# Weights by whole rows, four chunks first, and a second buffer of sums: a fused attention and feed-forward kernel on one core

## The chip, the cores and the metric

The kernel runs on one core of one Trainium2 chip. The metric is the device time of one execution in microseconds (us). Every comparison runs the changed kernel and the kernel before in turn on the same chip, and gives a 95% interval of the ratio. Faster or slower needs a difference of over 2%. A span is the time from the first to the last instruction of a profiled run. The granted clock is the share of TensorE's full clock that a profile shows as granted. A transfer is moved in packets (of w1, w2 and w3, one row or half row each: the profile before has 1536 packets of 4096 bytes, the half rows of w1 and w2) by the 16 DMA engines whose share the profile shows; a rate worked out from packets is 16 times the bytes of one over its mean time.

## The reference, cut to what matters

```python
# attention: q, k, v, f_logit are (4, 8, 768, 48)
f = 1.0 / (1.0 + np.exp(-f_logit))
for t in range(S):
    state = f[:, :, t, :, None] * state + np.einsum('bhd,bhe->bhde', k[:, :, t], v[:, :, t])
    y[:, :, t] = np.einsum('bhd,bhde->bhe', q[:, :, t], state)
# bridge to x of (3072, 384), then the feed-forward part
a = x @ w1                 # w1, w2: (384, 1024), float64
b = x @ w2
h = a * b @ w3             # w3: (1024, 1024), float64
return (h @ w_out).astype(np.float32)      # w_out: (1024, 384), float64
```

## The kernel before

The kernel works on 24 chunks of 128 tokens (attention) and on six blocks of 512 tokens (feed-forward). It multiplies w3 by w_out once (the "fold", 64 products of 384 columns; the trace has two matmul instructions for each product, 128 for these 64, so its counts are double) and then needs only up products (x with w1 and w2) and down products (a times b with the folded weights). From block 1 or 2 on it uses seven products in place of eight, which needs sums of the quarters of x and of the weights. A planner puts all work in order by priorities: a number given with each piece of work, lower first. This kernel has TensorE write its results into buffers called banks; four of them (f in the trace) serve the folds and the up and down products.

The weights arrive as 64-bit words and are decoded into float32: ScalarE and VectorE take them apart in a "raw" buffer and join them again. The 384 rows of w1 are the features of eight heads of 48. A chunk of rows on the 128 partitions is built of 96 rows from the upper part of the matrix and 32 from its end, so each piece of w1 or w2 needs two transfers, one into partitions 0 to 95 and one into 96 to 127:

```python
top, low = slice(0, 2 * D), slice(2 * D, P)          # 0:96 and 96:128
def source(w, kc0, kc1, half):
    cols = slice(half * NW, half * NW + NW)          # half a row: 512 words, 4096 bytes
    lo = HP * 2 * D - 2 * D
    n = P - 2 * D
    return (
        w[kc0 * 2 * D : kc1 * 2 * D, cols].rearrange("(kc p) c -> p kc c", p=2 * D),
        w[lo + kc0 * n : lo + kc1 * n, cols].rearrange("(kc p) c -> p kc c", p=n),
    )
due = {0: 2.0, 1: 26.0}
...
# the due times of the chunks of attention
return (0.0, 10.0, 22.0, 25.0)[u] if u < 4 else 45.0 + 14.5 * (u - 4)
...
# a leaves its bank into a buffer of its own; one buffer for the sums of x
s["a", jc, c0] = work.tile([P, TB], F32, name="a")
nc.scalar.copy(s["a", jc, c0][:, 0:nt], s["pu", jc, 0, c0][:, 0:nt])
...
xs = at(5120, 4, TH)
...
# a fold leaves its bank on VectorE; the down products rank by their block alone
return lambda: nc.vector.tensor_copy(wc[:, place_of(jc)], w3s["p", jc])
...
n0 = 100 * n + 90 + i
```

w3 and w_out need no split: each of their pieces is one transfer into all 128 partitions.

## Time and profile before

| what | before |
|---|---|
| time, median of 3 (lowest to highest) | 527.6 us (527.56 to 529.46) |
| span of the profiled run, and that same run's time | 528.7, 530.42 us |
| busy TensorE, VectorE, ScalarE, GpSimd | 94, 70, 30, 8% |
| first product of the fold starts | 87.6 us |
| first down product starts | 158.3 us |
| last matmul starts | 522.8 us |
| idle VectorE in the first 66 us | 15.1 us |

The prediction below reads the profile in detail. The list of transfer issues: its columns are the transfer, the queue, the count, the size of one, and the median time from issue to landing in us. These are lines of the kernel before; the list names the matrix of w1, w2 and w3 alike, and 1024 KB pieces are those of w3:

```profile
place<-in_w_dram SPq DMA_DIRECT2D x8, 1024.0 KB, 5.2
...
place<-in_w_dram SPq DMA_DIRECT2D x4, 768.0 KB, 10.4
place<-in_w_out_dram SPq DMA_DIRECT2D x4, 768.0 KB, 4.8
...
place<-in_w_dram SPq DMA_DIRECT2D x4, 384.0 KB, 13.0
```

A 768 KB piece of w_out into 128 partitions landed in 4.8 us; a 768 KB piece of w1 or w2 into 96 partitions took 10.4. The time to landing is more than the transfer's own: in the same list the 384 KB pieces took 13.0 us, longer than the 768 KB ones, so this alone proves nothing, but it is a warning that the length of a row is not the only difference between w1 and w3. The packet records of the same trace say more: the rows of w_out are shorter (3072 bytes), and yet their packets came at 310 GB/s (159 ns on average), those of w1 and w2 at 230.

### The profile page before, as it was taken

To read this page: it belongs to the slowest core of one execution; us is meant where nothing else is said; L and a number is where in the kernel's file an instruction comes from. 1 tells how busy PE (TensorE), PEld (TensorE's weight loads), DVE (VectorE), ACT (ScalarE), POOL (GpSimd) and SP (SyncE) were. 2 spreads that over 40 slices of the span, in tenths; PEclk is the share of its full clock that TensorE was granted. 3 is DMA by queue.
4 is the path that set the end of the run, shared out by engine and by line. 5 is a ranking of instruction groups with operands and counts; after the bars stand their busy time and mean duration, and the time that the engine had idled before them with its cause. 6 is when DMAs were issued, how large, how long until landed. Compare 5 with 4: busy or idle time off the path is not lost.

```text
span 528.7 us, 8629 instructions
## 1 busy us (share of the span) xinstructions
PE 497.6 (94%) x3306; PEld 423.3 (80%) x3306; DVE 369.4 (70%) x693; ACT 157.6 (30%) x328; POOL 40.0 (8%) x44
## 2 busy tenths in 40 slices
PE   3777999999999999999999999999999999999995
PEld 2666985666659988889889888898889888998884
DVE  6687999999998989364886657137673566456561
ACT  3646865663125465211351101401110111011000
POOL 5101001100012212000120000100000000000000
PEclk9988999999999999999999999999999999999999
DMA  6988886754113475000240001200013000000001
GB/s 168 217 215 222 259 262 207 235 197 135 29 47 114 130 223 153 30 1 16 56 141 30 1 0 31 76 30 1 0 30 92 2 0 1 31 30 1 1 17 51
DMA packets 29811, 46.02 MB, mean 87 GB/s; under 512 B 5440, under 2 KB 19264, under 8 KB 28736
## 3 DMA queue, kind: packets, MB, share of 16 engines
q1 hardware_dynamic: 29760, 45.37, 29.9%
q8 instruction: 28, 0.46, 0.4%
q14 instruction: 23, 0.19, 0.1%
HBM read 36.70 MB, written 4.72 MB: 78 GB/s over the span
## 4 chain that ended last, share of the span: by engine, by line
PE 77%; DMA 10%; DVE 5%; SPq 4%; POOL 1%; ACT 1%; issue 1%; DVEq 0%; POOLq 0%; ACTq 0%
PE f L481 57%; PE f L921 8%; DMA place<-in_w_dram 5%; PE pa L338 4%; PE py L382 3%; PE py L388 3%; DMA f<-in_f_logit_dram 2%; SPq L451 2%; PE pk L404 2%; PE pk L364 1%; DVE place L716 1%; DMA vt<-in_v_dram 1%; SPq L448 1%; DMA place<-in_w_out_dram 1%; DVE ab L623 0%
## 5 line engine op out<-in xcount | busy, mean ns | idle before, releaser
L481 PE MATMUL f<-xt,w 128*128 128x256 f32 (+2 forms) x696 | 163.6, 369 | 3.6 <-DVE w L868 3.6
L481 PEld LDWEIGHTS f<-xt,w 128*128 128x128 f32 x696 | 118.7, 194 | 25.3 <-issue 9.6
L481 PE MATMUL f<-place 128*128 128x192 f32 (+1 forms) x504 | 114.1, 350 | 2.9 <-DVE place L716 2.9
L481 PEld LDWEIGHTS f<-place 128*128 128x128 f32 x504 | 87.7, 190 | 9.8 <-DVE place L716 4.1
L353 POOL TENSOR_SCALAR_AFFINE_SELECT A<-A 128x1024 f32<-128x1024 f32 x24 | 33.0, 1374 | 296.5 <-ACT A L347 296.5
L921 PE MATMUL f<-place 128*128 128x384 f32 x128 | 43.0, 489 | 0.0
L584 ACT COPY a<-f 128x256 f32<-128x256 f32 x36 | 13.4, 372 | 97.3 <-PE f L481 96.4
L481 PE MATMUL f<-xt,place 128*128 128x256 f32 x144 | 37.1, 380 | 0.0
L481 PE MATMUL f<-wc,ab 128*128 128x192 f32 x192 | 36.5, 330 | 0.0
L921 PEld LDWEIGHTS f<-place 128*128 128x128 f32 x128 | 23.7, 190 | 15.7 <-issue 0.6
L608 DVE TENSOR_TENSOR place<-f,a 128x256 f32<-128x256 f32 x36 | 15.3, 425 | 28.9 <-PE f L481 28.9
L481 PEld LDWEIGHTS f<-wc,ab 128*128 128x128 f32 x192 | 31.7, 190 | 1.9 <-DVE ab L623 1.2
L338 PE MATMUL pa<-Q,K 48*128 48x128 f32 x384 | 29.8, 297 | 2.5 <-DVE K L329 2.3
L299 DVE TENSOR_TENSOR_SCAN fwd<-gate,floor 112x512 f32<-112x512 f32 x24 | 29.3, 1221 | 3.9 <-ACT gate L291 3.2
L338 PEld LDWEIGHTS pa<-Q,K 48*128 48x128 f32 x384 | 25.1, 199 | 8.6 <-issue 6.3
L321 DVE TENSOR_TENSOR_SCAN bwd<-gate,back 112x512 f32<-112x512 f32 x24 | 31.4, 1308 | 0.8
L382 PE MATMUL py<-A,vt 128*48 128x128 f32 (+1 forms) x384 | 27.9, 288 | 2.4 <-POOL A L353 1.5
L481 PEld LDWEIGHTS f<-xt,place 128*128 128x128 f32 x144 | 27.0, 189 | 3.7
L382 PEld LDWEIGHTS py<-A,vt 128*64 128x64 f32 (+1 forms) x384 | 21.8, 135 | 8.1 <-issue 5.2
L347 ACT COPY A<-pa 128x1024 f32<-128x1024 f32 x24 | 24.2, 1009 | 13.2 <-PE pa L338 13.1
L432 ACT ACTIVATE ys<-py 112x512 f32<-112x512 f32 x24 | 14.3, 596 | 38.0 <-PE py L388 25.4
L850 ACT ACTIVATE place<-place 128x1024 f32<-128x1024 f32 (+1 forms) x18 | 20.0, 1113 | 17.8 <-DMA place<-in_w_dram 9.3
(92 smaller groups left out, 622.3 us busy)
## 6 DMA issues: line engine op xcount, KB each, us to landing
place<-in_w_dram SPq DMA_DIRECT2D x8, 1024.0 KB, 5.2
f<-in_f_logit_dram SPq DMA_DIRECT2D x48, 96.0 KB, 2.8
q<-in_q_dram SPq DMA_DIRECT2D x48, 96.0 KB, 2.9
k<-in_k_dram SPq DMA_DIRECT2D x48, 96.0 KB, 2.8
vt<-in_v_dram SPq DMA_DIRECT2D x24, 192.0 KB, 2.9
out_dram<-o SPq DMA_DIRECT2D x24, 192.0 KB, 1.9
place<-in_w_dram SPq DMA_DIRECT2D x4, 768.0 KB, 10.4
place<-in_w_out_dram SPq DMA_DIRECT2D x4, 768.0 KB, 4.8
```

Of the source, the lines that this page charges most:

```text
L299: nc.vector.tensor_tensor_scan(s["P"], gate[u % 2][:, 0:NQ], floor, 0.0, ALU.mult, ALU.max)
L321: nc.vector.tensor_tensor_scan(s["R"][:, ::-1], gate[u % 2][:, NQ:0:-1], back[:, ::-1], 0.0, ALU.mult, ALU.max)
L338: nc.tensor.matmul(s["pa"][:, par, cols], lhsT=s["K"][rows(par), cols], rhs=s["Q"][rows(par), cols], start=True, stop=True,)
L347: nc.scalar.copy(s["A"].rearrange("p r h c -> p r (h c)"), s["pa"])
L353: nc.gpsimd.affine_select(out=a, in_=a, pattern=[[0, H], [1, C]], compare_op=ALU.is_ge, fill=0.0, base=0, channel_multiplier=-1,)
L382: nc.tensor.matmul(s["py"][64 * par : 64 * par + w, hp], lhsT=s["v"][:, h * D : h * D + w], rhs=s["A"][:, par, hp], start=(hp == 0), stop= ...
L388: nc.tensor.matmul(s["py"][:, hp], lhsT=sb[(u - 1) % 2][:, hp], rhs=s["Q"][:, hp * C : hp * C + C], start=False, stop=True, skip_group_che ...
L432: nc.scalar.activation(s["ys"], s["py"], AF.Copy, accum_out=ysum[:, u : u + 1])
L481: nc.tensor.matmul(out_, lhsT=lhs[i], rhs=rhs[i], start=start and i == 0, stop=i == len(lhs) - 1, skip_group_check=True,)
L608: nc.vector.tensor_tensor(ups["u3", k], q["Y"], q["a"], ALU.add)
L850: nc.scalar.activation(s["m"], s["hi"].bitcast(F32), AF.Abs)
L921: nc.tensor.matmul(w3s["p", jc], lhsT=w3s[jc][:, 0, kc * P : kc * P + P], rhs=wos[:, kc], start=(kc == 0), stop=(kc == KF - 1),)
```

## The change

Its intent: bring w1 and w2 by whole rows of 8192 bytes, have the first four chunks of attention (and so all of block 0's x) ahead of the weights, keep a in the place where the product goes, so that no buffer is waited for, move the copies of the folds to ScalarE, give the sums of x a second buffer, and rank the down products later, so that they run among the next block's up products. The diff, cut to its core:

```diff
-NW = 512
-NPE = 1
+NPE = 4
...
-        return (0.0, 10.0, 22.0, 25.0)[u] if u < 4 else 45.0 + 14.5 * (u - 4)
+        return (0.0, 1.0, 2.0, 3.0)[u] if u < 4 else 45.0 + 14.5 * (u - 4)
...
-    xs = at(5120, 4, TH)
+    xss = [at(a, 4, TH) for a in (5120, 12864)]
...
-                    s["a", jc, c0] = work.tile([P, TB], F32, name="a")
-                    nc.scalar.copy(s["a", jc, c0][:, 0:nt], s["pu", jc, 0, c0][:, 0:nt])
+                return lambda: nc.scalar.copy(a_b(jc)[:, cols], s["pu", jc, 0, c0][:, 0:nt])
...
-                last = [q[nm] for q in upq[-KF:] for nm in ("m5", "m6", "m7", "m3")] if i == 0 else []
+                last = [q[nm] for q in blk[n - 2].get("seven", []) for nm in ("m5", "m6", "m7", "m3")] if i == 0 else []
...
-            for c in range(UB):
-                part(c, c + 1, range(KH))
-            part(0, UB, range(KH, KF))
+            part(0, 2, range(KH))
+            part(2, 4, range(KH))
+            part(0, 4, range(KH, KF))
...
-            n0 = 100 * n + 90 + i
+            n0 = 100 * n + 90 + i + 60 * (n > 1) + 30 * (n == NB - 2)
...
+        for which, w in enumerate((w1, w2)):
+            for kc in range(KM):
+                loads_ = [
+                    (top, w[kc * 2 * D : kc * 2 * D + 2 * D].unsqueeze(1)),
+                    (low, w[lo + kc * n : lo + kc * n + n].unsqueeze(1)),
+                ]
+                ends = fetch(loads_, 1, (-26.0, -16.5)[which] + 0.1 * kc, [
...
-            return lambda: nc.vector.tensor_copy(wc[:, place_of(jc)], w3s["p", jc])
+            return lambda: nc.scalar.copy(wc[:, place_of(jc)], w3s["p", jc])
```

The diff also gives the decoding five raw buffers at first, in place of three, and decodes w1 and w2 in halves of 512 columns.

## The prediction

> **What bounds the kernel now.** I read four views: the busy rows in slices, the table by windows, the chain that ended last, and the gaps between matmuls in the trace. First the slices (40 slices of 13.2 us, busy tenths):
>
> ```profile
> PE   3777999999999999999999999999999999999995
> DVE  6687999999998989364886657137673566456561
> DMA  6988886754113475000240001200013000000001
> ```
>
> Three regimes show. Up to slice 5 (66 us) TensorE is not full while DMA is nearly full. From slice 4 to about slice 14 VectorE is full beside TensorE. After 215 us TensorE alone is full. The windows give the first two regimes in numbers (columns: window, its length, then busy us and instruction count of PE, PEld, DVE, ACT, POOL, then granted clock, DMA share, GB/s):
>
> ```profile
> 0.00:13.00 13.00, 4.01 (x36) 3.37 (x36) 8.87 (x18) 4.68 (x8) 7.19 (x21) 1.00 0.66 167
> 13.00:26.00 13.00, 9.61 (x88) 8.52 (x88) 7.94 (x10) 7.57 (x12) 2.29 (x2) 1.00 1.04 221
> 26.00:40.00 14.00, 9.71 (x75) 9.28 (x76) 12.29 (x20) 6.02 (x13) 0.00 (x0) 0.88 0.83 211
> 40.00:53.00 13.00, 9.56 (x95) 8.54 (x94) 9.58 (x15) 8.79 (x16) 1.79 (x2) 0.87 0.85 224
> 53.00:66.00 13.00, 13.00 (x136) 12.71 (x135) 12.23 (x21) 11.52 (x23) 1.00 (x1) 1.00 0.84 257
> 92.00:105.00 13.00, 12.98 (x88) 8.59 (x87) 12.72 (x18) 7.77 (x11) 1.40 (x1) 1.00 0.73 229
> ```
>
> In the first 66 us VectorE idles 15.1 us (4.1 + 5.1 + 1.7 + 3.4 + 0.8), with the DMA queues at 211 to 257 GB/s. The chain says what it waited for, then shows the PE-bound part (columns: start us, us, what):
>
> ```profile
> 6.46 8.87 DMA place<-in_w_dram
> 15.34 9.51 DMA place<-in_w_dram
> 30.49 9.29 DMA place<-in_w_dram
> ...
> 87.72 5.16 PE f L921 x16
> ...
> 158.41 2.80 PE f L481 x16
> ...
> 389.91 0.70 DVE place L716
> ...
> 448.32 0.70 DVE place L716
> ...
> 505.78 0.70 DVE place L716
> ```
>
> The w1/w2 pieces pace the start; 87.72 is the first product of the weight fold (w3 by w_out), 158.41 the first down product. Later there is only a step on VectorE at each block's end: the sums that the first down product needs.
>
> I then set TensorE's own work against the clock. Spacings between matmuls in the trace are about 0.43 us for 256 columns, 0.32 for 192, 0.85 for 512, 0.23 for 128, 0.645 for the fold's 384; the attention groups take 1.09 (pairs), 0.6 (turn, update), 1.02 (values), 1.06 (carry), from the chain. By these the program's order holds 485.3 us of TensorE work: 60.2 ahead of the first fold, 130.3 ahead of the first down product. So the lag (clock minus work) is 87.7 - 60.2 = 27.5 at the first fold, 158.4 - 130.3 = 28.1 at the first down product, and 523.1 - 485.3 = 37.8 at the last matmul; 5.6 us of evictions and store follow. Nearly three quarters of the lag is made before 66 us.
>
> [...] up to 130 us the 4096-byte packets of w1/w2 took 285 ns on average, the 8192-byte ones of w3 372 ns. On 16 engines that is 230 against 352 GB/s. [...] 949 ns for 768 and 1216 for 1024 elements of the sign step leave a fixed 148 ns. [...] Here four gaps of 0.90 us (at 321.7, 389.6, 448.0, 505.5) repeat, but they wait for operands rather than space.
>
> **The change part by part.**
>
> 1. Whole rows. w1/w2 are 6.29 MB: 1536 packets x 285 ns / 16 = 27.4 us of all engines become 768 x 372 / 16 = 17.9, so 9.5 us less DMA time in the stage that DMA limits. The decoding is in halves of 512: by the two-point fits 0.43 + 0.43 + 0.68 + 0.68 = 2.2 us each instead of 3.8 per 1024, which is 12 x 2.2 - 6 x 3.8 = 3.6 us more VectorE work (2.8 by spacing).
>
> 2. First four chunks ahead. Their 3.1 MB are what VectorE can start on (some 5 us of scans and scalings each, so about 20 us) while w1 lands. It should not stand idle for DMA as it does now. All four chunks' x is there by about 37 us: K of chunk 3 stands after 22 us of VectorE work, plus 5 us of start and waits makes 27, plus pairs 1.1, copy 1.0, mask 1.4, values and carry 2.1, ys 0.6, moving 1.5 + 0.5 and about 2 of queueing. w2 needs, with the 20 chunk tiles ahead of its end, about 13.5 + 17.9 us of DMA time at 0.9 share, so 37 us, and its last part waits for a raw buffer: first halves usable near 43. TensorE has w1 products until 45, as a is written in place and frees its bank.
>
> 3. Block 0 in halves of 256: 96 products of 128 columns (22.0 us) become 48 of 256 (20.6): -1.4 us. Total work is 483.9.
>
> 4. The new order puts all 24 products of 512 columns ahead of the folds (now 12 of them): 69.0 us of work precede the first fold. From x at 37 (25.1 done) that is 37 + 43.9 = 81. VectorE ahead of the first decoded w3 piece: six chunks of scans 6 x 2.72 = 16.3, 12 scalings x 0.62 = 7.4, states 3.7, 12 halves x 2.2 = 26.2, four w_out pieces x 2.9 = 11.6, w3 3.75, multiplications 4.7, memsets 1.9, so 75.6. Add 2.9 us of start, about 2 of waits for TensorE and 2.5 of operations stretched beside GpSimd: 83. The first fold then starts at 83.5, lag 14.5 (now 27.5).
>
> 5. Fold copies to ScalarE: 8 x 0.545 = 4.4 us off VectorE, 0.48 each on ScalarE, which has room (7.8 of 13 us busy in 92:105). From first to last fold end is 55.8 us of pure TensorE order now, and stays so: 139. VectorE's last w3 decode (118.4 of work + 9) is at 127, in time. The sums of the folded weights end near 144, the first down product starts at 147; lag 15.5.
>
> 6. Second buffer for the sums of x, and down products amid the next block: three of the four 0.90 gaps vanish as the sums run beside up products. The last vanishes too, since the printed order runs the last two blocks' downs in a row and block 5's sums fit beside block 4's downs: -3.6. Lag grows by 9.7 - 3.6 = 6.1 after the first down product.
>
> Sum: 483.9 + 15.5 + 6.1 + 5.6 = 511.1 us of span. The timed median is 1.1 below the profiled span (527.6 against 528.7), so 510; I add one for waits of the mixed order on four banks: 511.
>
> **The rivals.** (a) VectorE becomes the bound: it is full from 45 to 150 us, and the change gives it 3.6 and takes 4.4 + 1.1, so it gains only what it no longer idles. If it idles 12 instead of 7.5 us, the first fold is back at 88. But then TensorE still has done 8.8 us more work by then, and the first down product comes near 150, so about 515. Against: chunk data arrives before weights, and ScalarE's decoding is short. (b) Transfers hidden anyway: if the queue's issue rate (0.44 us per transfer, 20 for the first ten tiles) or the raw buffers pace w2, whole rows save little. If w2 stands at 52 instead of 43, TensorE idles 7 us: about 517. For it speaks that the profile's queue waits on earlier transfers; against, that the w1 products fill the time. (c) The down products amid the next block contend for the four banks with the up products and VectorE evictions: every 0.3 us per down quarter costs; I give it 2 us, 513. (d) Everything fits and the slack in 160:214 also shrinks: 506.
>
> **Range and chances.** Central 511, with the start uncertain by some 4 us each way and the ends by 2: 506 to 518. The 2% line is 527.6 x 0.98 = 517.0. Only (b), or (a) and (c) together, cross it: faster 0.84, same 0.15, slower 0.01.
>
> **What would show it.** Packets of w1/w2 near 370 ns; VectorE idle below 9 us up to 66 us; first fold at 81 to 86 and first down product at 145 to 150; no 0.9 us gap ahead of a block's first sum-fed product; lag at the last matmul near 22. Wrong if the first fold stays at 87 or later with VectorE full, if TensorE waits for w2 past 45 us, or if new gaps appear in the stretches where downs and ups mix.

The sum is 483.9 + 15.5 + 6.1 + 5.6 = 511.1 us of span, put at 511 us of time. The rates of packets beside the first cut are measured, but that the length of the rows makes the difference was the author's reading and not shown. The 2.5 us "stretched beside GpSimd" in part 4 are read from the trace before: in the first 83 us four VectorE operations that overlap a mask on GpSimd (L353) took 1.42, 0.86, 1.99 and 1.19 us (at 13.01, 45.85, 53.08 and 70.53), where their like took 0.69, 0.69, 1.23 and 0.36; a fifth mask, at 21.45, went with no such stretch.

## The result, and the profile after

The changed kernel is right and took 521.96 us (median of 4, 520.25 to 522.28) against 528.48 (527.56 to 529.46) for the kernel before in the same rounds: ratio 0.987, interval 0.9837 to 0.9902, so it is 1.3% faster, which counts as the same. A ratio is the mean time of one kernel's fast runs over that of the other's of the same rounds, so it is not quite the ratio of the medians quoted. The prediction of 511 (506 to 518) was 11 us too low.

The busy slices of the changed kernel (40 slices of 13.0 us, tenths):

```profile
PE   3788999999999999999999999999999999999995
...
DVE  6767899999999999664796766526665567665541
...
DMA  6999767764233464300241001210012000000011
```

TensorE stands at 8 instead of 7 in the third and fourth slices, but the DMA row is at 9 from the second to the fourth, fuller than before. The windows of the changed kernel (columns as in the prediction's windows):

```profile
13.00:26.00 13.00, 9.78 (x84) 8.52 (x86) 9.62 (x14) 7.10 (x16) 2.29 (x2) 0.85 1.04 225
26.00:40.00 14.00, 10.90 (x110) 9.51 (x107) 10.04 (x18) 8.26 (x16) 2.77 (x2) 0.90 1.04 225
40.00:53.00 13.00, 12.00 (x90) 10.15 (x89) 9.22 (x20) 8.00 (x18) 0.00 (x0) 1.00 0.89 192
53.00:66.00 13.00, 12.47 (x56) 10.23 (x56) 12.22 (x27) 8.79 (x18) 0.00 (x0) 1.00 0.70 209
```

The DMA share is full (1.04) in two windows, at 225 GB/s. VectorE is idle for 3.4 to 4.0 us in each of the first three. In the packet records of 6 to 57 us, the 8192-byte packets of w1 and w2 took 579 ns on average; before, the 4096-byte ones took 285. Double the packet in double the time is the same rate: 226 and 230 GB/s. The chain of the changed kernel shows what that did (start us, us, what):

```profile
20.69 12.05 DMA place<-in_w_dram
32.76 12.16 DMA place<-in_w_dram
45.36 7.36 DMA place<-in_w_dram
...
56.60 18.82 PE f L479 x68
...
93.90 5.36 PE f L937 x16
...
156.72 2.80 PE f L479 x16
```

The transfers of w1 and w2 still pace the start up to 52.7 us, and the products that need w2 start at 56.60 instead of about 43. The first fold starts at 93.8 (predicted 83.5; before 87.6, with less TensorE work ahead of it), the first down product at 156.7 (predicted 147). From there on the change did what was hoped: from the first down product to the start of the last matmul the kernel before took 364.5 us, the changed one 357.6, and none of the four 0.90 us gaps at a block's end is left. (The 0.90 is counted from start to start of two matmuls, less their spacing; the views show the same gap as 0.73 or 0.74 us of idle time.) The transfer list of the changed kernel:

```profile
place<-in_w_dram SPq DMA_DIRECT2D x8, 1024.0 KB, 5.0
...
place<-in_w_dram SPq DMA_DIRECT2D x6, 768.0 KB, 11.5
...
place<-in_w_out_dram SPq DMA_DIRECT2D x4, 768.0 KB, 4.9
```

Rows of w1 and w2 are now as long as those of w3, and the 96-partition pieces still take over twice as long to land as the w_out pieces of the same 768 KB (11.5 against 4.9 us).

### The profile page after: what moved, and what is told of

It is laid out like the page before. It is cut to its first block, busy times and chain, and to the rows that moved or that the text cites. A ratio compares the mean times of both kernels' runs of the same rounds, so it can differ in the third digit from the quotient of the medians.

```text
span 520.6 us, 8446 instructions
## 1 busy us (share of the span) xinstructions
PE 495.4 (95%) x3210; PEld 419.1 (81%) x3210; DVE 369.7 (71%) x701; ACT 161.6 (31%) x340; POOL 39.3 (8%) x44
## 4 chain that ended last, share of the span: by engine, by line
PE 79%; DMA 9%; DVE 7%; issue 1%; POOL 1%; SPq 1%; ACT 0%; DVEq 0%; ACTq 0%; POOLq 0%
PE f L479 62%; PE f L937 8%; DMA place<-in_w_dram 6%; PE pa L336 3%; PE py L380 2%; PE py L386 2%; DMA vt<-in_v_dram 2%; DVE bwd L319 2%; DVE fwd L297 2%; PE pk L402 1%; PE pk L362 1%; DVE Q L313 1%; DMA q<-in_q_dram 0%; DMA f<-in_f_logit_dram 0%; DVE K L327 0%
## 5 line engine op out<-in xcount | busy, mean ns | idle before, releaser
L479 PE MATMUL f<-xt,w 128*128 128x256 f32 (+1 forms) x600 | 160.5, 397 | 0.5 <-DVE w L881 0.4
L479 PEld LDWEIGHTS f<-xt,w 128*128 128x128 f32 x600 | 112.9, 190 | 25.5 <-issue 10.0
L479 PE MATMUL f<-wc,ab 128*128 128x192 f32 x192 | 35.3, 327 | 0.0
L297 DVE TENSOR_TENSOR_SCAN fwd<-gate,floor 112x512 f32<-112x512 f32 x24 | 30.9, 1287 | 3.0 <-ACT gate L289 1.8
L380 PE MATMUL py<-A,vt 128*64 128x128 f32 (+1 forms) x384 | 27.9, 290 | 2.2 <-DMA vt<-in_v_dram 1.8
L864 ACT ACTIVATE place<-place 128x512 f32<-128x512 f32 (+2 forms) x24 | 21.1, 879 | 20.3 <-DMA place<-in_w_dram 13.3
L867 ACT ACTIVATE place<-place 128x512 f32<-128x512 uint32 (+2 forms) x24 | 21.1, 880 | 10.9 <-DMA place<-in_w_dram 6.3
## 6 DMA issues: line engine op xcount, KB each, us to landing
place<-in_w_dram SPq DMA_DIRECT2D x6, 768.0 KB, 11.5
```

Of the source, the lines that this page charges most:

```text
L297: nc.vector.tensor_tensor_scan(s["P"], gate[u % 2][:, 0:NQ], floor, 0.0, ALU.mult, ALU.max)
L380: nc.tensor.matmul(s["py"][64 * par : 64 * par + w, hp], lhsT=s["v"][:, h * D : h * D + w], rhs=s["A"][:, par, hp], start=(hp == 0), stop= ...
L479: nc.tensor.matmul(out_, lhsT=lhs[i], rhs=rhs[i], start=start and i == 0, stop=i == len(lhs) - 1, skip_group_check=True,)
L864: nc.scalar.activation(m, hi.bitcast(F32), AF.Abs)
L867: nc.scalar.activation(lo.bitcast(F32), lo, AF.Copy, bias=2.0, scale=2.0**-51)
```

## The experiments

The theory to test: w1 and w2 come at 225 to 230 GB/s because each piece is split by partitions into 96 and 32, not because of the length of their rows. In the expectations P stands for this theory and the other letters for rivals: that row length matters in itself (R), that the order with the chunks first was the mistake (O), and others described where they stand. Fifteen runs followed (three of them controls or repeats), in four sets, each set on one chip and with its own runs of the kernel before. All ratios are of fast runs; the one slow run, of the kernel before in the third set (533.63 us), moves that set's median of 528.66 by under 0.02. Three of the kernels put wrong rows of w1 and w2 on the partitions; their results are wrong, their traffic and arithmetic are those of a right kernel.

### One transfer over 128 partitions, wrong rows on purpose

```diff
-                loads_ = [
-                    (top, w[kc * 2 * D : kc * 2 * D + 2 * D].unsqueeze(1)),
-                    (low, w[lo + kc * n : lo + kc * n + n].unsqueeze(1)),
-                ]
+                loads_ = [(slice(0, P), w[kc * P : kc * P + P].unsqueeze(1))]
```

> The changed kernel, but every 1 MB piece of w1 and w2 comes as one transfer of 128 rows to 128 partitions instead of 96 rows to partitions 0-95 and 32 rows to 96-127 (wrong rows on purpose, so the result is wrong; bytes, row length and all instruction orders are those of the changed kernel). Theory P (the partitions that a transfer reaches limit its rate[...]): 8 KB packets of w1/w2 fall from 580 ns to 370-450 ns, the products that need w2 start near 47 us instead of 56.6, time 511 to 515 us. Rival C (the start is limited to about 225 GB/s by everything that is loaded at once, whatever the partitions): packets stay above 520 ns, time 520 to 523 us.

Measured: 514.22 us against 526.74 (ratio 0.9761, 0.9723 to 0.9799). The 8192-byte packets of the start took 338 ns, less than the 370 to 450 expected, and the last of w2's first halves is decoded at 46.3. A window of this kernel:

```profile
13.00:26.00 13.00, 10.19 (x110) 8.78 (x111) 11.77 (x16) 9.68 (x21) 3.13 (x3) 1.00 1.03 385
```

The share is full as before, but the rate is 385 GB/s instead of 225. The first fold starts at 84.8, the first down product at 147.6, VectorE idles 7.0 us up to 66: close to the numbers that the prediction had named (83.5, 147 and 7.5).

### Two transfers of 64 partitions, wrong rows on purpose

```diff
-                    (top, w[kc * 2 * D : kc * 2 * D + 2 * D].unsqueeze(1)),
-                    (low, w[lo + kc * n : lo + kc * n + n].unsqueeze(1)),
+                    (slice(0, 64), w[kc * P : kc * P + 64].unsqueeze(1)),
+                    (slice(64, P), w[kc * P + 64 : kc * P + P].unsqueeze(1)),
```

> The changed kernel, but each piece comes as rows 0-63 to partitions 0-63 and rows 64-127 to partitions 64-127, two equal transfers of 512 KB (wrong rows on purpose). Theory P: [...]no better than 96 + 32: packets 540-620 ns, time 520 to 524 us. Rival S (what is slow is the uneven 96 + 32 split or a row count that is no power of two): packets near 380 ns, time 511 to 515 us. Rival C: as the changed kernel, 520 to 523 us.

Measured: 521.28 us (ratio 0.9895, 0.9857 to 0.9933), as slow as the changed kernel; packets of 589 ns, first fold at 92.0. The same window of this kernel:

```profile
13.00:26.00 13.00, 9.83 (x104) 8.59 (x105) 10.31 (x14) 7.84 (x17) 2.47 (x3) 1.00 1.03 222
```

An even split with no small transfer in it is held at the same rate, 222 GB/s here against 225. It is the cut across the partitions that costs, not the unevenness of 96 and 32. The next run has as many transfers (twelve of 512 KB) and moves its packets at 334 GB/s, so it is not their number either.

### 128 partitions, two half rows, wrong rows on purpose

```diff
-                nc.sync.dma_start(raw.rearrange("p (a m) -> p a m", a=a)[place_], src.bitcast(U32))
+                to, from_ = raw.rearrange("p (a m) -> p a m", a=a)[place_], src.bitcast(U32)
+                ...
+                for half in range(2):
+                    cut = slice(half * total, half * total + total)
+                    nc.sync.dma_start(to[:, :, cut], from_[:, :, cut])
...   (and the single 128-partition source of the first experiment)
```

> The changed kernel, but each piece comes as two transfers of 128 rows, the left and the right 4 KB of every row (wrong rows on purpose). Theory P: fast as with one transfer, 4 KB packets at 185-225 ns, time 511 to 515 us. Rival R (4 KB row parts are slow as such, which the prediction believed): packets 285 ns, w2 late, time 519 to 523 us.

Measured: 513.9 us (ratio 0.9753, 0.9716 to 0.9791), the same as with whole rows. The 4096-byte packets took 196 ns (334 GB/s). So half rows over all partitions do as well for the time as whole ones, and whole rows, the change's stated aim, were worth nothing measurable in the time here. In rate they do count for something, 388 GB/s against 334.

### Right rows, 96 and 32, in half rows

The same cut of the columns, with the 96 and 32 rows of the changed kernel (order: both halves of the 96, then both of the 32). The result is right.

> The changed kernel with the right rows, 96 + 32, but every transfer cut into the left and the right 4 KB of its rows; result right. Theory P: the rate does not care about the row length, packets 285 ns for 4 KB, time within 1 us of the changed kernel (520 to 523 us). Rival R (whole rows did help, and something else eats it): slower by 3 us or more.

Measured: 517.67 us (ratio 0.9826, 0.9784 to 0.9868), packets of 4096 bytes at 255 ns (257 GB/s), first fold at 89.5. I had expected no change. The rate is indeed above the 226 of the changed kernel, and the time is 3.6 us below the even split on the same chip. But the changed kernel's own ratio was 0.987 in its first trial and 0.9841 in a second one below, so what it gained is 0.2 to 0.4% of the time, no more than the interval is uncertain by. Why smaller pieces come faster was not tried.

### Right rows, 96 and 32 in turn, in half rows

```diff
+            for half in range(2):
+                cut = slice(half * total, half * total + total)
+                for place_, src in loads_:
+                    to = raw.rearrange("p (a m) -> p a m", a=a)[place_]
+                    nc.sync.dma_start(to[:, :, cut], src.bitcast(U32)[:, :, cut])
```

> Right rows; every piece of w1/w2 as four transfers in the order left half of 96 rows, left half of 32 rows, right half of 96, right half of 32 (w_rowhalves had both halves of 96 first). Theory P: finer alternation[...] lets neighbours overlap more: packets 240 to 255 ns for 4 KB, time 515 to 518 us. Rival: only the number of transfers counts, then the same as w_rowhalves within 0.5 us, or slower by queue time.

Measured: 519.33 us against 529.28 (ratio 0.9838, 0.9784 to 0.9893), runs from 516.27 to 522.21; packets at 260 ns (252 GB/s), slower than the 240 to 255 expected, and the time is above the 515 to 518 expected. It is no better than the other order, and the scatter does not let the two be ranked.

### The old rank of the down products

```diff
-            n0 = 100 * n + 90 + i + 60 * (n > 1) + 30 * (n == NB - 2)
+            n0 = 100 * n + 90 + i
```

> The changed kernel without one part: the down products of a block have their old rank, right after their own block's up products. Theory G (the gain of the changed kernel is mostly the vanished 0.9 us gaps at block ends, 4.2 us, plus 1.4 us less TensorE work and 2.6 us of start): the 0.90 us gaps ahead of the first sum-fed down product are back at three or four block ends and the time rises by 3 to 4 us over the changed kernel, to about 525. Rival N (the order of the downs is worth nothing, the gaps went for another reason): within 1 us of the changed kernel.

Measured: 520.48 us (ratio 0.9867, 0.9815 to 0.9919). One 0.90 us gap came back, at 495.3, and three stayed away. From the first down product to the last matmul it took 359.2 us; the unaltered changed kernel took 357.6 and 357.8 in its two profiles. The rank is worth about 1.5 us, less than the 3 to 4 that I expected.

### The old rank, and a single buffer for the sums of x

```diff
-    xss = [at(a, 4, TH) for a in (5120, 12864)]
+    xss = [at(5120, 4, TH)] * 2
...
-                last = [q[nm] for q in blk[n - 2].get("seven", []) for nm in ("m5", "m6", "m7", "m3")] if i == 0 else []
+                last = [q[nm] for q in upq[-KF:] for nm in ("m5", "m6", "m7", "m3")] if i == 0 else []
...   (and the old rank)
```

The single buffer with the new rank could not be tried: the planner finds no order for it.

> As u_down, and the sums of x have a single buffer again (with the single buffer alone the planner finds no order). Against u_down this tells what the second buffer does. Theory G: nothing of its own, within 1 us of u_down; its worth is that it lets the downs move. Rival X: the single buffer makes the sums of x wait for the last up products of the block before, another 1 to 3 us at five block starts.

Measured: 525.98 us (ratio 0.9951, 0.9923 to 0.9979), on the same chip 4.6 us (by means) above the kernel with the old rank alone, whose order of loads is the same. All the gaps are back. I had expected at most 1 us. TensorE's timeline in this kernel (start, us, engine, line, what; in brackets the idle time before, and what ended it), at the end of a block:

```profile
382.75 1.73 PE L479 MATMUL f<-wc,ab 128*128 128x192 f32 x8
385.22 4.17 PE L479 MATMUL f<-place 128*128 128x192 f32 x24 [0.74 <-DVE place L714]
```

and in the kernel with the old rank and two buffers:

```profile
381.51 1.46 PE L479 MATMUL f<-wc,ab 128*128 128x192 f32 x8
382.81 1.03 PE L479 MATMUL f<-xt,w 128*128 128x256 f32 x4
383.67 4.50 PE L479 MATMUL f<-place 128*128 128x192 f32 x26
```

The first down products of a block need only a and b; those that follow need sums, made on VectorE (L714). With one buffer the next block's up products cannot start until the last of this block's are done with the sums of x, so there is nothing to run and TensorE waits. With two, up products of the next block (f<-xt,w) stand in between and the wait is hidden. So the second buffer does most of the work that the prediction shared between the buffer and the rank. The three more gaps are 2.7 of the 4.6 us; 0.74 us of waiting for a transfer of v at 335.0 and a longer wait for a chunk at 192.5 make up most of the rest. The prediction read the gaps as waits for operands rather than space: TensorE does wait for operands there, but it has nothing else to run for want of space.

### The old due times of the first four chunks

```diff
-        return (0.0, 1.0, 2.0, 3.0)[u] if u < 4 else 45.0 + 14.5 * (u - 4)
+        return (0.0, 10.0, 22.0, 25.0)[u] if u < 4 else 45.0 + 14.5 * (u - 4)
```

> The changed kernel with the old due times of the first four chunks, so that the pieces of w1 and w2 are asked for right after chunk 0 and the other three chunks come between or behind them. Theory P (all of it passes[...] at about 225 GB/s, so the order moves little as long as TensorE needs both): the products that need w2 start earlier but chunk 1 to 3 come later; VectorE idles 15 us or more up to 66 us; time within 3 us of the changed kernel, 519 to 525. Rival O (putting chunks first was the mistake that ate the gain): 511 to 516 us.

Measured: 536.93 us (ratio 1.0187, 1.0123 to 1.0251). First up product at 44.4, first fold at 99.4, VectorE idle for 18.0 us up to 66. I had expected at most 3 us; on this chip it is 16 us more than the kernel with the old rank. With weights this slow, the chunks are, as I read it, what the engines live on meanwhile. Having them first is worth some 16 us in this kernel, though at 2% the verdict against the kernel before is unclear, and the rival that called it the mistake falls.

### The changed kernel again, as a control

Unaltered, on the chip of the next three.

> The changed kernel once more, unaltered, as the control for the other three on the same chip. Both theories: 519 to 523 us, ratio to the kernel before 0.984 to 0.990; 8192-byte packets of w1 and w2 at 570 to 590 ns, the first fold of w3 between 90 and 94 us (kernels with the same order of loads have shown 90.6 to 93.8 on different chips).

Measured: 519.59 us against 528.66 (ratio 0.9841, 0.9786 to 0.9896), 2.4 below the first result. Its first fold starts at 91.2 instead of 93.8. Its packets took 547 ns (240 GB/s), less than the 570 to 590 expected, and the granted clock was 1.00 in all windows up to 66 us, where the first profile showed 0.85 and 0.90 in two of them.

### The rows in the order of the chunks: a right kernel with 128-partition transfers

```diff
+    rows_ = np.concatenate([
+        np.r_[kc * 2 * D : kc * 2 * D + 2 * D, (HP - 1) * 2 * D + kc * n : (HP - 1) * 2 * D + kc * n + n] for kc in range(KM)
+    ])
...
-        "w1": words(moe_w1),
-        "w2": words(moe_w2),
+        "w1": words(moe_w1[rows_]),
+        "w2": words(moe_w2[rows_]),
...   (and the single 128-partition source of the first experiment)
```

The function that lays out the inputs, which already turns q, k, f_logit and w3, also puts the rows of w1 and w2 in the order in which the chunks want them. It does no arithmetic.

> The changed kernel with the rows of w1 and w2 laid by the layout function in the order of the chunks, so that each piece is one transfer over 128 partitions; the result stays right. Theory P (the split into 96 and 32 partitions[...] is what held w1 and w2 at half rate): packets of 8192 bytes at 330 to 370 ns, first fold at 84 to 86 us, 512 to 516 us, ratio 0.974 to 0.980. Rival (the gain of the wrong-rowed kernel came from wrong data or another accident): packets above 500 ns, first fold near 92, 519 us or more.

Measured: right, 513.71 us (513.1 to 515.48) on the control's chip, 5.9 us below the control's median; against the kernel before the ratio is 0.9742 (0.9684 to 0.9801), unclear at 2%. Packets took 342 ns (383 GB/s, against 240 in the control), and the first fold started at 84.9. A second trial on another chip, with five rounds:

> The kernel with the reordered rows once more, unaltered, as the control for the next run on the same chip: 512 to 516 us, ratio 0.971 to 0.980, granted clock 1.00 in all windows up to 66 us, first fold 84 to 86 us.

Measured: 514.15 us (513.06 to 515.86) against 528.30, ratio 0.9727 (0.9694 to 0.976): faster. Packets of 359 ns (365 GB/s), first fold at 85.1, first down product at 147.9, VectorE idle for 7.3 us up to 66. Two windows, the chain, and the transfers of this second trial:

```profile
13.00:26.00 13.00, 10.33 (x108) 8.91 (x108) 11.41 (x15) 9.36 (x21) 3.08 (x3) 1.00 1.03 354
26.00:40.00 14.00, 13.56 (x142) 11.77 (x143) 13.55 (x29) 12.34 (x27) 1.09 (x1) 1.00 0.66 216
```

```profile
14.15 10.58 DMA place<-in_w_dram
...
40.84 25.86 PE f L479 x102
...
85.17 5.36 PE f L934 x16
...
147.98 2.80 PE f L479 x16
```

```profile
place<-in_w_dram SPq DMA_DIRECT2D x14, 1024.0 KB, 5.5
```

The DMA share falls to 0.66 from 26 us on, VectorE is full from there (13.55 of 14), one stretch of weight transfer is left in the chain's start where there were three, and TensorE runs 102 matmul instructions of up products in a row from 40.84. This version beats both kernels: 514.15 against 528.30 for the kernel before; on the control's chip 513.71 against 519.59 for the change as it was given.

### The kernel before with rows in the order of the chunks

The same order of rows and 128-partition transfers in the kernel before, with its half rows and its order of work kept.

> The kernel before with that same order of rows and 128-partition transfers, its half-row columns and its order of work kept. Theory P: its 4096-byte packets of w1 and w2 fall from 285 to 190 to 210 ns, so the old kernel's start was held by the split as well; first fold 3 to 6 us earlier than its 87.6, and 522 to 526 us (ratio 0.989 to 0.996). Rival D (the old start is bound by VectorE and by the late due times of w2, and the packets' rate is hidden): packets fall, but the first fold stays within 1.5 us and so does the time. Rival R (short rows are slow in themselves): packets stay near 285 ns.

Measured: 525.26 us against 528.66, ratio 0.9977 with an interval of 0.9897 to 1.0058, with one run at 529.77: a small gain could not be told from none. Packets took 198 ns, and the first fold started at 80.4. Again with five rounds:

> The kernel before with the rows in the order of the chunks, again, because three rounds left its gain unclear (0.9977, 0.9897 to 1.0058, with one outlier) while its profile showed the first fold 7 us earlier than the profile of before. If the split paced the old start too: ratio 0.986 to 0.994, first fold 80 to 83 us, and the granted clock up to 66 us above that of before. If the gain is eaten later: first fold as early, but a ratio of 0.996 or more.

Measured: 525.01 us against 528.30, ratio 0.9937 (0.9903 to 0.997). Packets of 4096 bytes at 195 ns instead of 285; first fold at 81.2 instead of 87.6, VectorE idle for 8.4 us instead of 15.1. (The profile of before showed a granted clock of 0.88 and 0.87 in two windows of the start, this one 0.88 in one, so part of the 6 us may be clock.) The time fell by 3.3 us only; the profile of before is of a run of 530.42 us, above that kernel's median of 527.6, so 6 us overstates it. So the split held the old start too, for 0.6% of the time. By means on this chip, the rest of the change is worth 11.1 us (2.1%) once both kernels have fast transfers.

### The fold copies back on VectorE

```diff
-            return lambda: nc.scalar.copy(wc[:, place_of(jc)], w3s["p", jc])
+            return lambda: nc.vector.tensor_copy(wc[:, place_of(jc)], w3s["p", jc])
...
-            folds.append(plan.add("ACT", 0.48, folded(jc), fp[-1:], -10, frees=fp[-1:]))
+            folds.append(plan.add("DVE", 0.6, folded(jc), fp[-1:], -10, frees=fp[-1:]))
```

> The changed kernel with the copies of the folds of w3 from PSUM put back on VectorE. The prediction said that this move buys nothing by itself because TensorE has no wait there: within 1.5 us of the control, last fold within 1 us. Rival: VectorE is the nearly full engine between 60 and 150 us, so the copies delay its sums and casts: the last fold 2 us later or more, and 3 to 5 us on the time.

Measured: 522.75 us (ratio 0.9896, 0.9835 to 0.9957), 3 above the control. But its profile fell into its slowest run, with a granted clock of 0.67 and 0.83 in two windows of the start and the first fold 3.8 us late, before any copy was made. So the same edit ran once more, on the kernel with the reordered rows:

> That kernel with the fold copies put back on VectorE. Here the start is fed and the granted clock should stay at 1.00, so the dip that confounded the first trial of this edit (0.67 and 0.83 in two windows) is gone. If the move of the copies buys nothing, as the prediction's fifth part said: within 1 us of the control. If VectorE, full between 45 and 150 us, is hindered by 8 copies of some 0.55 us: the last fold 1 us later or more and 2 to 4 us on the time.

Measured: 516.8 us (516.09 to 517.77) against 514.15 (513.06 to 515.86) for its control: 2.7 us by means, and no run of the one reaches the other's. The granted clock was 1.00 in every window up to 215 us. Yet the folds are not late: the last one starts at 133.7 against 135.7, the first down product at 146.2 against 147.9. The time is lost between 175 and 205 us. TensorE's timeline there, with the copies on VectorE:

```profile
178.03 0.57 PE L362 MATMUL pk<-ident,K 112*128 112x112 f32 x4 [0.76 <-DVE K L327]
...
190.83 1.16 PE L336 MATMUL pa<-Q,K 48*128 48x128 f32 x16 [1.72 <-DVE Q L313]
...
194.90 0.60 PE L362 MATMUL pk<-ident,K 112*128 112x112 f32 x4 [0.36 <-DVE S L417]
...
202.79 1.16 PE L336 MATMUL pa<-Q,K 48*128 48x128 f32 x16 [0.72 <-DVE G L412]
```

and of the control, which has one such wait in the stretch:

```profile
186.97 0.60 PE L362 MATMUL pk<-ident,K 112*128 112x112 f32 x4 [1.21 <-DVE S L417]
```

The four waits sum to 3.56 us against 1.21. With the copies on VectorE, the work of the chunks of attention is put off (TensorE starts the tenth chunk, pa, at 151.9 against 141.0), and VectorE owes it when TensorE reaches the chunks 40 us after the folds. My expectation had the size (2 to 4 us) right in its second branch and the place (a late last fold) wrong.

## Why the prediction was wrong

**The step that failed: part 1.** It took "768 x 372 / 16 = 17.9, so 9.5 us less DMA time": the packet time of w3's 8192-byte rows for those of w1 and w2. They measured 579 ns, so 768 of them need 27.8 us on 16 engines, against 27.4 before. Nothing was saved. The two rates that the prediction set side by side, 230 and 352 GB/s, differed in two things at once, the row length and the split across partitions, and it put all of it down to the row length. Its own trace had the counter-example, w_out's shorter rows at 310 GB/s. The experiments separate them: 64 + 64 partitions with long rows, 223 GB/s; 128 partitions with short rows, 334 GB/s; 128 with long rows, 388.

Every kernel whose packets are given here fits: those with split pieces stayed between 223 and 257 GB/s, those with 128 partitions between 331 and 388. What is shown is the cost of the split. By what mechanism it costs that, no run shows, and why 96 and 32 (226 and 240 GB/s in whole rows) come little or no faster than 64 and 64 (223) stays open.

**What followed from it.** Part 2 counted w2 "usable near 43"; the products with w2 started at 56.60. Part 4 put the first fold at 83.5 and part 5 the first down product at 147; they were at 93.8 and 156.7. Rival (b) had the outcome ("If w2 stands at 52 instead of 43"), but argued for it with the issue of transfers and the raw buffers, and priced it at 517.

**What was right.** With the transfers repaired and nothing else altered, the steps come out: VectorE idle for 7.3 us (7.5, in rival (a)), first fold at 85.1 (83.5), first down product at 147.9 (147), last matmul at 505.9 (the sum, 511.1 less 5.6, is 505.5), span 511.4 and 512.2 in two profiles (511.1). Putting chunks ahead, and products ahead of folds, was thus worked out soundly. Two things made this come out closer than it should. The products with w2 could start at 46.5, not near 43 (the prediction's 37 for the landing is 31.4 over 0.9, so 34.9, and some 2 us that it does not name; the last piece landed at 40.9): the last piece of w2 was asked for at 36.6, after 7.3 us of waiting for VectorE to free a raw buffer, but TensorE had other products until then. And the terms of part 6 cancelled.

**Part 6** was near in sum, by luck in part, and wrong in its shares. The gaps went, and the lag after the first down product grew by 5.2 us where 6.1 was predicted (357.6 us on the clock less 352.4 of work, which is the 483.9 in all less the 131.5 that the prediction has ahead of the first down product, 147 less 15.5). But the prediction counted 3.6 us for buffer and rank together, and taking them out cost more: some 4.6 for the second buffer of sums and some 1.5 for the rank. With both out, the lag grows by 11.3 us (363.7 less 352.4) and not by the 9.7 of the kernel before, so the rest of the changed kernel loses some 1.6 us there. No part of the prediction has this loss. Where it lies was not tried; but the chain of the changed kernel runs over VectorE from 173.5 to 194.8 us, where that of the kernel before runs over TensorE:

```profile
173.49 0.99 DVE place L714
...
193.93 0.90 DVE G L412
195.16 0.60 PE pk L362 x4
```

**Part 5** gave the copies on ScalarE no gain of their own. The move is worth 2.7 us in the kernel with the reordered rows, collected not at the folds but at 178 to 203 us, where VectorE would still owe the work. The sum has no term for it: the prediction took the growth of lag from the kernel before, where TensorE has no such wait.

**The step from span to time.** The prediction said that the timed median lies 1.1 below the profiled span. It compared the median of some runs with the span of another: the profiled run itself was timed at 530.42, 1.7 above its span of 528.7. All later runs agree, with 1.7 to 1.8 (513.24 against 511.4). So a right span of 511.4 is a time of 513.2.

**The 11 us, added up.** The split: 5.9 (control less repaired kernel, medians on one chip). The repaired kernel lies 2.7 above the prediction (513.71 less 511), the step from span to time most of all. The rest, 2.4, is what the first result lies above the control, which ran in another set; the first profile had slower packets (579 against 547 ns) and a lower granted clock in its start (0.85 and 0.90 in two windows, against 1.00) than the control, and its first fold was 2.6 us later, but which of the two caused which was not tried.

## What to carry to other kernels

When two rates in a profile differ, list everything in which the two transfers differ before putting it down to one; here the list of issues had a piece of equal size, shorter rows and other partitions, at half the time (4.8 against 10.4 us), that would have told. Try a layout of the weight in which each piece is one transfer over all 128 partitions, with its rows reordered on the way in if need be: here that was worth 5.9 us, and the length of its rows nothing that shows (514.22 us with whole rows, 513.9 with half ones). And work taken off a full engine may pay off far from where it stood (here 2.7 us, at 178 to 203 us, while the last fold starts at 133.7), so look for it where that engine is next waited for.
